# Block B's last output groups as two row halves in two PSUM banks, copied and added by VectorE

## The chip, the cores and the metric

The kernel runs on one NeuronCore of one Trainium2 chip, in one launch. The metric is the device time of that launch in microseconds. Three runs of the kernel before took 1746.45, 1746.89 and 1746.9 us, so the median is 1746.89 us. Five engines work side by side, each through its own queue in order: TensorE (PE, with its weight loads shown as PEld), VectorE (DVE), ScalarE (ACT), GpSimd (POOL), and SyncE (SP), which here only issues DMAs. Engines wait for one another through semaphores. TensorE writes its results to PSUM, which has 8 banks of 512 fp32 columns in each of 128 partitions.

## The reference

Two attention blocks stand side by side, each with 2048 positions, 640 features and 32 heads of 20. Block A attends to 8 positions at a stride of 2; block B is full softmax attention. Cut to what matters for this change, block B is:

```python
qkv = ((x @ wqkv).reshape(B, S, 3, H, Dh)).transpose(2, 0, 3, 1, 4)
q, k, v = qkv[0], qkv[1], qkv[2]
scores = jnp.einsum("bhqd,bhkd->bhqk", q, k) * (Dh ** -0.5)
p = softmax(scores, axis=-1)
o = jnp.einsum("bhqk,bhkd->bhqd", p, v)
return o.transpose(0, 2, 1, 3).reshape(B, S, D) @ wo      # the output projection
```

The change is in the last line, `@ wo`, of block B.

## The kernel before

**Number format.** An fp32 operand of a projection is split into a high and a low part of TensorE's fp32r format (`split`), and a product is three passes: high x high, high x low, low x high (`PASSES`). With 640 features in `KC = 5` chunks of 128, one output group of 128 rows x 320 columns is 15 matmuls that add up in one PSUM bank.

**Stages.** Projections of A and B come first, then the V projections with the first maxima of B, then block B's main loop of 512 steps (`NS`). A step is one group of four heads, one of four query chunks of 512 (`qc`), and one of 16 key blocks of 128. A step has 4 score matmuls (128 keys x 512 queries), 4 exponentials on ScalarE, and 4 value matmuls of 32 output columns each, which put the four heads into four 32-partition strips of one bank (a trace shows each value matmul as two). VectorE takes row maxima for a later step; GpSimd does block A's attention. Of the 512 steps all but the last `TAIL = 24` stand in an order that is written out as a string (`ORDER`). The last 24 are a plain loop at the end of the function: by then VectorE has no maxima left.

**The plain loop.** Each step issues its 8 score and exponential instructions (`b_qk`). Every odd step then issues the value matmuls of two earlier steps (`b_pv`), and takes one waiting job from the list `fill`. These jobs are `out_group(qc, n)`: one 128 x 320 piece of block B's output. Two steps therefore form a period that repeats: 8 score matmuls, 16 value matmuls (as a trace counts them), 15 output matmuls. On ScalarE the period is 8 exponentials, the copy of the value bank into `more` (or `braw`), and the copy of the output bank into `ro` (`store_rows`). SyncE then sends `ro` to `ob`. Jobs that are left over run after the loop, followed by the eight output groups of the last query chunk.

**PSUM banks.** Banks 4 to 7 serve in pairs through `wide()`, and the second half of each step's score matmuls (`pl = 1`) uses them. Banks 0 to 3 are handed out first in, first out:

```python
def bank():
    n = given.pop(0) if given else free.pop(0)
    t = psb[:, n]
    taken[id(t)] = (None if loop[0] is not None and loop[1] else n, t)
    return t

def give(t):
    n = taken.pop(id(t))[0]
    if n is not None:
        free.append(n)
```

`bank()` and `give()` run while the program is written, not on the chip. Each call takes the bank that was taken four calls earlier, and the matmul that writes it gets a semaphore wait for whichever engine reads that older content. In a period, in this order, the first step's scores take two (call them S1 and S2; S3 and S4 are in wide banks), the second step's scores take two (S5 and S6; S7 and S8 are wide), the value matmuls take one, and the output group takes one. So S5 reuses the bank of the last value sum, and S6 that of the last output group.

**Row halves elsewhere.** The V projection already has a form with halves of 64 rows (`v_matmuls` with `r`), where two 64-row matmuls, one on rows 0 to 63 and one on rows 64 to 127, write different banks. Score matmuls also use 62 of 64 rows.

In the profile every recorded instruction has line 71, since the helper class `InOrder` issues them all; they are told apart by tile names: `ps_st` is PSUM, `bq,bk` score matmuls, `e,vb` value matmuls, `ww,xn` and `ww,xl` the projections with 320 columns (output groups, in the plain loop; `xl` is the fifth chunk), `e` exponentials, `ro` output rows.

Of the kernel before, what the change touches and what calls it, by code (L numbers as in the profile page):

```python
# [10 lines left out]
F32 = mybir.dt.float32  # L11
F32R = mybir.dt.float32r
AF = mybir.ActivationFunctionType
ALU = mybir.AluOpType
# [8 lines left out]
KC = 5  # L23
# [7 lines left out]
PASSES = ((0, 0), (0, 1), (1, 0))  # L31
# [7 lines left out]
HALF = 64  # L39
# [3 lines left out]
NS = NG * NQC * NKB  # L43
# [32 lines left out]
def attention_pair(ctx, tc, xa, wqk_a, wv_a, wo_a, xb, wqk_b, wv_b, wo_b, oa, ob):  # L76
# [3 lines left out]
    sb = ctx.enter_context(tc.tile_pool(name="sb", bufs=1))  # L80
    ps = ctx.enter_context(tc.tile_pool(name="ps", bufs=1, space=PS))
    dr = ctx.enter_context(tc.tile_pool(name="dr", bufs=1, space=bass.MemoryType.DRAM))
    pe, dve, act, gp, sp = (InOrder(tc, e) for e in (nc.tensor, nc.vector, nc.scalar, nc.gpsimd, nc.sync))
# [5 lines left out]
    def after(n, fn, *args):  # L89
        due.setdefault(now[0] + n, []).append((fn, args))  # L90
# [32 lines left out]
# [12 lines that stand above are left out]
# [27 lines left out]
    def split(hi, lo, src, tag="stg", second=None, first=None):  # L162

        t = sb.tile([128, 640 if tag == "stg" else 1024], F32, tag=tag, bufs=3 if tag == "stg" else PB, name="stg")
        raw = t[:, :src.free_size()] if len(src.shape) == 2 else (
            t[:, :src.shape[1] * src.shape[2]].rearrange("p (k c) -> p k c", c=src.shape[2]))
        sp.dma_start(raw, src)

        def parts():
            (first or act.copy)(hi, raw)  # L170
            (second or dve).tensor_tensor(lo, raw, hi.bitcast(F32), ALU.subtract)
        after(odd(wait[0]), parts)
# [8 lines left out]
    def chunk(t, xi, k):  # L181
        return t[k // (KC - 1)][:, xi, k % (KC - 1)]
# [90 lines left out]
    def store_rows(p, dst):  # L273
        r = sb.tile([128, 320], F32, tag="r", bufs=4, name="ro")
        act.copy(r, p[:, :320])
        if id(p) in taken:
            give(p)
        after(1, sp.dma_start, dst, r)
# [231 lines left out]
    for n in range(NA):  # L510
        nxt = None
        for t in range(NT):
            if n == 0 and t < 4:
                p = first[t]
            else:
                p = next(banks)
# [64 lines left out]
    for m in range(0, 10, 2):  # L581
        nxt = []
        for n in range(4):
            for j in range(2):
                p = next(banks)
                for k in range(KC):
                    for i, (wi, xi) in enumerate(PASSES):
                        pe.matmul(p, WB[j][:, wi, k], chunk(XB[n], xi, k), start=(k == 0 and i == 0),
                                  stop=(k == KC - 1 and i == 2))
# [154 lines left out]
    def b_qk(i):  # L744
        for pl in range(2):
            w = wide() if pl else None
            ps2 = [bank() for _ in range(2)] if w is None else [w[:, 0], w[:, 1]]
            for r in range(2):
                s_matmul(i, pl, r, ps2[r])
            for r in range(2):  # L750
                s_exp(i, pl, r, ps2[r])
                if w is None:
                    give(ps2[r])

    def b_pv(i):
        u, kb = divmod(i, NKB)
        g, qc = divmod(u, NQC)
        n, part = divmod(kb, 2)
        if part == 0:
            accs[u] = bank()  # L760
        acc = accs[u]
        for j in range(GH):
            pe.matmul(acc[32 * j:32 * j + 32, :], stacks[g][2][:, kb, j * VC:j * VC + 32], P[i][j % 2][:, j // 2],
                      start=(part == 0), stop=(part == 1))
        del P[i]
        if part == 0:
            return
        del accs[u]
        if n == 0:
            raws[u] = sb.tile([128, 512], F32, tag="raw", bufs=3, name="braw")  # L770
            act.copy(raws[u], acc)
        else:
            more = spare[n % 2][:, n // 2 % 2]
            act.copy(more, acc)
            after(2, pool, raws[u], raws[u], more, ALU.add)
        give(acc)
        if kb == NKB - 1:
            last = g == NG - 1
            normalize(raws.pop(u), g, qc * 512, *((2, 3) if last else (5, 8)), (lambda: out_last(qc)) if last else None)
# [64 lines left out]
    outs_b = {}  # L844

    def out_first(qc):

        o = columns(2)
        outs_b[qc] = o
        for k in range(KC - 1):  # L850
            after(1 + 2 * k, split, chunk(o, 0, k), chunk(o, 1, k),
                  ot_b[k * 128:(k + 1) * 128, qc * 512:(qc + 1) * 512], "stg", gp, gp.tensor_copy)

    def out_last(qc):
        o = outs_b[qc]
        k = KC - 1
        split(chunk(o, 0, k), chunk(o, 1, k), ot_b[k * 128:(k + 1) * 128, qc * 512:(qc + 1) * 512])
        if qc < NQC - 1:
            for n in range(8):
                after(3 + (1 + (qc < 2)) * n, fill.append, lambda n=n: out_group(qc, n))  # L860

    def out_matmuls(p, qc, n, ks):
        for k in ks:
            for i, (wi, xi) in enumerate(PASSES):
                pe.matmul(p[:, :320], chunk(outs_b[qc], xi, k)[:, n // 2 * 128:n // 2 * 128 + 128], WO_b[n % 2][wi][:, k],
                          start=(k == 0 and i == 0), stop=(k == KC - 1 and i == 2))

    def out_dst(qc, n):
        r0 = qc * 512 + n // 2 * 128
        return ob[r0:r0 + 128, n % 2 * 320:n % 2 * 320 + 320]  # L870

    def out_group(qc, n):
        p = bank()
        out_matmuls(p, qc, n, range(KC))
        store_rows(p, out_dst(qc, n))
        if n == 7 and qc + 2 < NQC:
            out_first(qc + 2)

# [112 lines left out]
    fill = []  # L991

    WO_b = []
# [4 lines left out]
    def begin(i):  # L998

        g, sub = divmod(i, NQC * NKB)  # L1000
        if sub == (1 if g else 2) and g + 1 < NG:
            k_loads, q_loads = b_pieces(g + 1) if g else ([], q1_loads)
            for n, fn in enumerate(k_loads + q_loads + [lambda g=g + 1: v_piece(g, 0, NKB)]):
                after(1 + (n if n < 8 else 2 * n - 7), fn)
        if i in (NS - 56, NS - 40):
            out_first((i - NS + 56) // NKB)
        tick()
        if loads and (i % 2 or i < 12):
            loads.pop(0)()
        if turn_jobs and turn_jobs[0][0] <= now[0]:  # L1010
            run_jobs(turn_jobs, 1)
        if soft_jobs and soft_jobs[0][0] <= now[0]:
            run_jobs(soft_jobs, 1)
        if done_a and done_a[0][0] <= 0 and len(turned) + len(turn_jobs) < 2 and not loads and i > 10:
            a_turn(*done_a.pop(0)[1:])
        turn_parts()
        gp.us = max(gp.us, (i - 1) * STEP)
        while i >= A_FROM and gp.us < i * STEP + AHEAD:
            if next(a_work, 0) is False:
                break  # L1020
            if not a_work.gi_frame:
                for d in done_a:
                    d[0] -= 1
                break
# [70 lines left out]
    i = 0  # L1095
# [25 lines left out]
    for i in range(NS - TAIL, NS + LAG):  # L1121
        begin(i)
        if i < NS:
            b_qk(i)
        if i % 2:
            b_pv(i - LAG - 1)
            b_pv(i - LAG)
            if fill:
                fill.pop(0)()


    qc = NQC - 1
# [13 lines left out]
    for n, p in enumerate(last):  # L1146
        out_matmuls(p, qc, n, (KC - 1,))
        r = sb.tile([128, 320], F32, tag=("r", "p")[n > 1], bufs=(4, PB)[n > 1], name="ro")
# [38 lines left out]
```

## Time and profile before

| | us |
|---|---|
| median of three runs | 1746.89 |
| profiled execution | 1745.1 |
| its span | 1742.9 |
| PE busy | 1726.1 |
| DVE busy | 1349.3 |
| ACT busy | 1337.3 |
| POOL busy | 1271.9 |
| first and last output group in the plain loop's periods | starts at 1629.9 and 1690.4 |

The span is that of the instructions; the execution takes 2.2 us more than its span. PE is busy 99% of it, but a matmul's row covers its whole stay in a pipelined array, so a busy PE may still be waiting to start the next one; start times tell more. The granted TensorE clock is 1.00 in the windows around the change. In the stretch from 1660 to 1670 us ScalarE is busy 9.43 of 10 us, VectorE 0.00, and GpSimd 1.30.

### The profile page before, as it was taken

To read this page: it belongs to the slowest core of one execution; us is meant where nothing else is said; L and a number is where in the kernel's file an instruction comes from. 1 tells how busy PE (TensorE), PEld (TensorE's weight loads), DVE (VectorE), ACT (ScalarE), POOL (GpSimd) and SP (SyncE) were. 2 spreads that over 40 slices of the span, in tenths; PEclk is the share of its full clock that TensorE was granted. 3 is DMA by queue.
4 is the path that set the end of the run, shared out by engine and by line. 5 is a ranking of instruction groups with operands and counts; after the bars stand their busy time and mean duration, and the time that the engine had idled before them with its cause. 6 is when DMAs were issued, how large, how long until landed. Compare 5 with 4: busy or idle time off the path is not lost.

```text
span 1742.9 us, 34666 instructions
## 1 busy us (share of the span) xinstructions
PE 1726.1 (99%) x12711; PEld 1011.2 (58%) x12711; DVE 1349.3 (77%) x1818; ACT 1337.3 (77%) x2658; POOL 1271.9 (73%) x1125
## 2 busy tenths in 40 slices
PE   9999999999999999999999999999999999999999
PEld 8988888989635544444444443444444445444568
DVE  3113232888899999999999999999999999999300
ACT  4323223232599999999999999999999999999981
POOL 0000950999899999999999999999999953545242
PEclk9999999999999999999999999999999999999999
DMA  6447878657754263445435433543642532111123
GB/s 226 120 139 242 304 258 261 219 183 219 207 152 133 91 175 119 130 127 148 128 121 158 141 126 106 176 136 110 168 137 96 142 90 55 43 36 52 34 75 113
DMA packets 194435, 248.29 MB, mean 142 GB/s; under 512 B 89308, under 2 KB 114396, under 8 KB 193272
## 3 DMA queue, kind: packets, MB, share of 16 engines
q1 hardware_dynamic: 193688, 245.41, 46.6%
q8 instruction: 100, 1.64, 0.4%
q14 instruction: 71, 0.58, 0.1%
q10 hardware_dynamic: 576, 0.66, 0.1%
HBM read 181.08 MB, written 64.91 MB: 141 GB/s over the span
## 4 chain that ended last, share of the span: by engine, by line
PE 73%; POOL 17%; DMA 4%; issue 3%; DVE 2%; ACT 1%; SPq 1%; POOLq 0%; ACTq 0%; DVEq 0%
PE ps_st L71 73%; POOL akv L71 9%; POOL braw L71 4%; DVE mx L71 2%; POOL ao L71 1%; DMA stg<-xa 1%; SPq L71 1%; DMA mdr<-mtr 1%; DMA bq<-qb_d 1%; POOL ww L71 1%; POOL al L71 1%; ACT e L71 1%; DMA s_d<-braw 1%; POOL xn L71 0%; DMA s_d<-sm 0%
## 5 line engine op out<-in xcount | busy, mean ns | idle before, releaser
L71 DVE TENSOR_REDUCE mx<-ps_st 128x1 f32<-128x512 f32 (+1 forms) x1500 | 1227.5, 877 | 72.5 <-PE ps_st L71 61.4
L71 ACT ACTIVATE e<-ps_st 128x512 f32<-128x512 f32 x2048 | 1067.3, 630 | 32.5 <-PE ps_st L71 19.6
L71 PE MATMUL ps_st<-bk,bq 60*128 60x512 f32 x2048 | 555.1, 436 | 0.5 <-DVE mx L71 0.4
L71 PE MATMUL ps_st<-bq,bk 62*128 62x512 f32 x2048 | 548.7, 431 | 3.5 <-ACT e L71 1.8
L71 PE MATMUL ps_st<-e,vb 128*32 128x512 f32 x4096 | 543.1, 604 | 0.5
L71 PEld LDWEIGHTS ps_st<-bq,bk 62*128 62x128 f32 x2048 | 276.6, 184 | 401.6 <-ACT e L71 250.2
L71 POOL TENSOR_TENSOR braw<-braw,more 128x512 f32<-128x512 f32 x224 | 288.3, 1287 | 85.6 <-ACT more L71 85.1
L71 PEld LDWEIGHTS ps_st<-bk,bq 60*128 60x128 f32 x2048 | 257.9, 184 | 102.9 <-DVE mx L71 45.1
L71 POOL TENSOR_TENSOR akv<-akv,aq 128x1280 f32<-128x1280 f32 x64 | 188.4, 2944 | 166.4 <-DMA akv<-ka_d 166.3
L71 POOL TENSOR_TENSOR akv<-akv 128x640 f32<-128x640 f32 (+3 forms) x304 | 282.6, 930 | 14.7
L71 ACT COPY ro<-ps_st 128x320 f32<-128x320 f32 (+2 forms) x172 | 73.9, 465 | 185.9 <-PE ps_st L71 104.0
L71 PE MATMUL ps_st<-ww,xn 64*128 64x320 f32 (+1 forms) x1776 | 188.1, 311 | 6.5 <-POOL xn L71 2.4
L71 PEld LDWEIGHTS ps_st<-ww,xn 64*128 64x128 f32 (+1 forms) x1776 | 175.6, 187 | 22.6 <-ACT e L71 8.3
L71 PEld LDWEIGHTS ps_st<-e,vb 128*32 128x32 f32 x4096 | 82.2, 108 | 149.9 <-issue 77.1
L71 POOL TENSOR_TENSOR akv<-akv,al 128x1280 f32<-128x1280 f32 x64 | 151.6, 2368 | 0.1
L71 ACT COPY more<-ps_st 128x512 f32<-128x512 f32 x224 | 136.7, 610 | 4.0 <-POOL braw L71 2.0
L71 PE MATMUL ps_st<-xn,w 128*128 128x512 f32 x480 | 115.8, 390 | 0.0
L71 PEld LDWEIGHTS ps_st<-xn,w 128*128 128x128 f32 x480 | 90.1, 188 | 19.4
L71 POOL TENSOR_TENSOR xn<-stg,xn 128x512 fp32r<-128x512 f32 (+1 forms) x30 | 53.8, 1804 | 62.8 <-ACT xn L71 61.5
L71 PE MATMUL ps_st<-ww,aot 64*128 64x320 f32 x960 | 99.2, 308 | 0.0
L71 ACT CAST pr<-ps_st 128x512 fp32r<-128x512 f32 x40 | 23.5, 587 | 98.7 <-PE ps_st L71 93.0
L71 PEld LDWEIGHTS ps_st<-ww,aot 64*128 64x128 f32 x960 | 91.0, 186 | 4.6 <-DVE mx L71 0.5
(65 smaller groups left out, 1042.3 us busy)
## 6 DMA issues: line engine op xcount, KB each, us to landing
akv<-ka_d SPq DMA_DIRECT2D x128, 320.0 KB
akv<-va_d SPq DMA_DIRECT2D x128, 320.0 KB
kb_d<-pr SPq DMA_DIRECT2D x20, 512.0 KB
qb_d<-pr SPq DMA_DIRECT2D x20, 512.0 KB
bk<-kb_d SPq DMA_DIRECT2D x16, 640.0 KB
bq<-qb_d SPq DMA_DIRECT2D x64, 160.0 KB
stg<-xb SPq DMA_DIRECT2D x16, 512.0 KB
rb<-s_d SPq DMA_DIRECT2D x128, 64.0 KB
```

The source lines that it names most:

```text
L71: return self.tc.keep_in_program_order(op(*a, **k))
```

## The change

An output group that is taken from `fill` inside the loop while `i < NS` is no longer 15 matmuls of 128 rows into one bank, but 30 matmuls of 64 rows: 15 pairs, of which one half (rows 0 to 63) adds up in one bank and the other (rows 64 to 127) in a second. VectorE copies the first bank into `ro` and then adds the second bank to it. ScalarE's copy of these groups is gone. Both banks are taken before the first matmul and given back after the add has been issued. Groups that run with or after step `NS` keep the old form.

```diff
-                after(3 + (1 + (qc < 2)) * n, fill.append, lambda n=n: out_group(qc, n))
+                after(3 + (1 + (qc < 2)) * n, fill.append, lambda *halves, n=n: out_group(qc, n, *halves))
...
-    def out_group(qc, n):
-        p = bank()
-        out_matmuls(p, qc, n, range(KC))
-        store_rows(p, out_dst(qc, n))
+    def out_group(qc, n, halves=False):
+        if halves:
+            ps2 = [bank(), bank()]
+            for k in range(KC):
+                for i, (wi, xi) in enumerate(PASSES):
+                    for h, p in enumerate(ps2):
+                        rows = slice(h * HALF, h * HALF + HALF)
+                        pe.matmul(p[:, :320], chunk(outs_b[qc], xi, k)[rows, n // 2 * 128:n // 2 * 128 + 128], WO_b[n % 2][wi][rows, k],
+                                  start=(k == 0 and i == 0), stop=(k == KC - 1 and i == 2))
+            r = sb.tile([128, 320], F32, tag="r", bufs=4, name="ro")
+            dve.tensor_copy(r, ps2[0][:, :320])
+            dve.tensor_tensor(r, ps2[1][:, :320], r, ALU.add)
+            for p in ps2:
+                give(p)
+            after(1, sp.dma_start, out_dst(qc, n), r)
+        else:
+            p = bank()
+            out_matmuls(p, qc, n, range(KC))
+            store_rows(p, out_dst(qc, n))
...
-                fill.pop(0)()
+                fill.pop(0)(i < NS)
```

Twelve groups take the new form: one in each of the loop's twelve periods. A period now calls `bank()` seven times instead of six, so the reuse shifts: S1 takes the bank of the last S6, S2 that of the last value sum, S5 that of the first half and S6 that of the second half. The value sum takes the bank of this period's S1, the two halves take those of this period's S2 and S5.

TensorE's queue before, over one period in the plain loop; `x2` counts equal instructions in a row, the brackets name the engine whose semaphore is waited for:

```order
L71 MATMUL ps_st<-ww,xn 128x320 [waits Activation_49]
L71 MATMUL ps_st<-ww,xn 128x320 x11
L71 MATMUL ps_st<-ww,xl 128x320 x3
L71 MATMUL ps_st<-bq,bk 128x512 [waits Activation_49] x2
L71 MATMUL ps_st<-bq,bk 128x512 x2
L71 MATMUL ps_st<-bq,bk 128x512 [waits Activation_49] x2
L71 MATMUL ps_st<-bq,bk 128x512 x2
L71 MATMUL ps_st<-e,vb 32x512 [waits Activation_49]
L71 MATMUL ps_st<-e,vb 32x512 x7
```

And the same place now:

```order
L71 MATMUL ps_st<-ww,xn 128x320 [waits Activation_49] x2
L71 MATMUL ps_st<-ww,xn 128x320 x22
L71 MATMUL ps_st<-ww,xl 128x320 x6
L71 MATMUL ps_st<-bq,bk 128x512 [waits Activation_49] x2
L71 MATMUL ps_st<-bq,bk 128x512 x2
L71 MATMUL ps_st<-bq,bk 128x512 [waits DVE_49] x2
L71 MATMUL ps_st<-bq,bk 128x512 x2
L71 MATMUL ps_st<-e,vb 32x512 [waits Activation_49]
L71 MATMUL ps_st<-e,vb 32x512 x7
```

The 15 output matmuls have become 30, the second of them with a wait of its own, and the second pair of waiting score matmuls (S5 and S6) now waits for VectorE instead of ScalarE.

VectorE's queue now, at the fifth to seventh changed group, with buffer numbers; `xl` is the low part of another chunk and `sm` a reciprocal of softmax sums, which stood there before without the rows of `ro`:

```order
L71 COPY ro_18999<-ps_st_66 128x320 [waits DMAHW0_49,PE_49,Activation_49]
L71 TENSOR_TENSOR ro_18999<-ps_st_66,ro_18999 128x320 [waits DVE_49,PE_49,Activation_49]
L71 TENSOR_TENSOR xl_18271<-stg_18933,xl_18271 128x512 [waits DMAHW5_49,Activation_49]
L71 COPY ro_19067<-ps_st_66 128x320 [waits DMAHW7_49,PE_49]
L71 TENSOR_TENSOR ro_19067<-ps_st_66,ro_19067 128x320 [waits DVE_49,PE_49,Activation_49]
L71 COPY ro_19131<-ps_st_66 128x320 [waits DMAHW0_49,PE_49,Activation_49]
L71 TENSOR_TENSOR ro_19131<-ps_st_66,ro_19131 128x320 [waits DVE_49,PE_49,Activation_49]
L71 RECIPROCAL sm_18966<-sm_18966 128x16 [waits DMAHW1_49]
```

Each add waits for VectorE's own copy before it. SyncE's sends of these twelve `ro` tiles stand where they stood and wait for VectorE instead of ScalarE.

## The prediction

> **What bounds the kernel now.** I read the chain of waits first, cut to the stretch of the change, since it names what the end depends on.
>
> ```profile
> 3 pieces in order of time: start us, us, what
> 1639.67 99.15 PE ps_st L71 x688
> 1738.82 0.02 issue
> 1738.84 0.42 ACT ro L71
> ```
>
> From 1639.67 us to the last copy the end is set by TensorE alone: 688 matmuls in a row, no other engine between them. Whatever delays a matmul in the changed periods therefore delays the end, unless TensorE stood waiting later. So I looked next at the timeline of the last 22 us.
>
> ```profile
> 1721.05 14.24 PE L71 MATMUL ps_st<-ww,xn 128*128 128x320 f32 x96
> 1728.49 0.69 DVE L71 TENSOR_TENSOR xl<-stg,xl 128x512 fp32r<-128x512 f32 x1 [26.35 <-ACT xl L71]
> 1735.12 3.68 PE L71 MATMUL ps_st<-ww,xl 128*128 128x320 f32 x24
> ```
>
> The last chunk (`xl`) is ready at 1728.49 + 0.69 = 1729.18 and is first used at 1735.12: 5.9 us to spare. The transfers behind it start from the value matmuls at the loop's end, so they move with TensorE, and the spare time stays. Nothing there absorbs a delay or a gain.
>
> Then the timeline of one period of two steps, with the two rows that give its length, and the weight load of S6:
>
> ```profile
> 1632.29 1.31 PE L71 MATMUL ps_st<-bq,bk 62*128 62x512 f32 x8
> ...
> 1643.29 1.31 PE L71 MATMUL ps_st<-bq,bk 62*128 62x512 f32 x8
> 1643.39 0.43 ACT L71 COPY ro<-ps_st 128x320 f32<-128x320 f32 x1 [0.57 <-PE ps_st L71]
> 1643.82 4.03 ACT L71 ACTIVATE e<-ps_st 128x512 f32<-128x512 f32 x8
> 1643.87 0.29 PEld L71 LDWEIGHTS ps_st<-bq,bk 62*128 62x128 f32 x3
> 1644.53 1.92 PE L71 MATMUL ps_st<-e,vb 128*32 128x512 f32 x16
> ...
> 1646.38 2.03 PE L71 MATMUL ps_st<-ww,xn 128*128 128x320 f32 x12
> 1647.65 0.67 ACT L71 COPY more<-ps_st 128x512 f32<-128x512 f32 x1
> 1648.25 0.60 PE L71 MATMUL ps_st<-ww,xl 128*128 128x320 f32 x3
> 1648.46 1.29 POOL L71 TENSOR_TENSOR braw<-braw,more 128x512 f32<-128x512 f32 x1 [4.22 <-ACT more L71]
> 1648.78 1.31 PE L71 MATMUL ps_st<-bq,bk 62*128 62x512 f32 x8
> ...
> 1687.27 1.31 PE L71 MATMUL ps_st<-bq,bk 62*128 62x512 f32 x8
> ```
>
> Ten periods lie between the rows at 1632.29 and 1687.27: 5.498 us each. One period is scores 1.24 (1643.29 to 1644.53), values 1.85 (to 1646.38), output group 2.40 (to 1648.78). ScalarE waits 0.57 us in it, so it is not the bound. But see what stands at the seam: the `ro` copy ends at 1643.39 + 0.43 = 1643.82, and the weight load of S6, which reuses the bank that was copied, starts at 1643.87, 0.05 later. Counted from the first score matmul, S6 starts at +0.58. Eight scores spread over 1.24 us would put the sixth at about +0.5 or later anyway. So today the evacuation of the output bank just keeps pace with the scores, with nothing in hand.
>
> **The change, part by part.** All times below are counted from S1's start in the new period.
>
> *ScalarE loses the `ro` copy* (12 x 0.43 = 5.2 us). It is off the chain, since ScalarE had 0.57 us of idle time ahead of each copy. I cost the gain at nothing; the exponentials start with S1's result as before. ScalarE's own period shrinks to 4.03 + 0.67 = 4.7 us, further below TensorE's.
>
> *15 matmuls of 128 rows become 30 of 64 rows.* The V projection shows this form between score matmuls of the same 64-row kind:
>
> ```profile
> 419.74 1.93 PE L71 MATMUL ps_st<-ww,xn 64*128 64x320 f32 x24
> 421.51 0.60 PE L71 MATMUL ps_st<-ww,xl 64*128 64x320 f32 x6
> 421.95 0.69 PE L71 MATMUL ps_st<-bk,bq 60*128 60x512 f32 x4
> ```
>
> Thirty take 421.95 - 419.74 = 2.21 us, so two halves cost what one full matmul costs, about 0.147 us per pair. The present 2.40 us are 15 such slots plus 0.19 for entering from the value matmuls and leaving to the scores. Leaving becomes cheap, as here; entering from the values stays. I take 2.31, halfway, with 2.21 and 2.40 as ends: a gain of 0.09 a period. The Trainium skill says as much (TensorEngine Tiling (Array Packing), Key Properties): switching the tiling mode drains the array, while going from one tile to another of the same mode does not. The change removes one of three switches in a period; by that rule alone, with the whole 0.19 gone, eleven periods would gain 2.1 us, and the rule speaks for the change.
>
> *Two dependent VectorE instructions take the place of one ScalarE copy,* and S5 and S6 wait for them. Their prices:
>
> ```profile
> L71 DVE TENSOR_TENSOR pr<-ps_st,pr 128x512 fp32r<-128x512 f32 x40 | 27.6, 690 | 85.3 <-ACT pr L71 85.3
> L71 DVE TENSOR_TENSOR wd<-stg,wd 128x256 fp32r<-128x256 f32 x6 | 2.5, 418 | 0.0
> L71 DVE COPY ro<-ps_st 128x320 f32<-128x320 f32 x4 | 2.0, 491 | 7.7 <-PE ps_st L71 7.7
> L71 DVE TENSOR_TENSOR ww<-stg,ww 128x320 fp32r<-128x320 f32 x2 | 1.0, 483 | 0.0
> 1624.72 2.36 DVE L71 TENSOR_REDUCE mx<-ps_st 128x2 f32<-128x1024 f32 x2
> 1627.12 0.22 DVE L71 TENSOR_REDUCE mx<-mx 128x16 f32<-128x64 f32 x1
> 1627.13 0.19 PEld L71 LDWEIGHTS ps_st<-bq,bk 62*128 62x128 f32 x2 [0.95 <-DVE mx L71]
> 1627.43 0.21 DVE L71 STREAM_TRANSPOSE mtr<-mx 128x32 f32<-128x32 f32 x1
> ```
>
> The copy has its own row: 0.49. The add has none; the nearest is the 320-column one from SBUF, 0.48, with 0.42 (256 columns) and 0.69 (512 columns, one operand in PSUM as here) as ends. I take 0.48, the same column count. Handing over costs 0.04 from TensorE to the evacuating engine (last output matmul ends 1648.25 + 0.60 = 1648.85; one period earlier the copy started 0.04 after it), 0.09 from one VectorE instruction to a dependent one (1627.34 to 1627.43), and 0.05 from VectorE to TensorE (1627.08 to 1627.13).
>
> Step by step: the last pair of halves ends at 421.51 + 0.60 = 422.11, 0.16 after the first score matmul. So the copy runs from +0.20 to +0.69, and S5 starts at +0.74. The add runs from +0.78 to +1.26, and S6 starts at **+1.31** instead of +0.58. TensorE's queue is in order: behind S6 stand S7, S8 and all value matmuls. From S6 to the values is 0.66 now (1643.87 to 1644.53), so the values start at +1.97, the output group 1.85 later at +3.82, and the next S1 at +3.82 + 2.31 = **+6.13**, against 5.50. That is 0.63 us lost per period.
>
> *The other new waits.* The second half's bank is that of this period's S5, whose exponential is ScalarE's fifth. Eight follow each other at (1647.65 - 1643.82) / 8 = 0.48 us and end 4.03 after the first starts, at +0.53; the fifth ends three slots before that, at +3.1, ahead of +3.82. Hidden. S1 waits for the last S6's exponential and S2 for the copy of the value sum, which start even earlier against the longer period. The `xl` subtraction and the reciprocal on VectorE stand between groups, and VectorE has over 4 us free per period. *SyncE* sends `ro` when the add is done, some 0.7 us later in the period than now, and its later DMAs queue behind that; the earliest that matters is the chunk for the last groups, with the 5.9 us above. *GpSimd* is not touched.
>
> *Sum.* Eleven of the twelve groups are followed by scores; the twelfth is followed by values alone and is costed at nothing (its bank is needed only a group later). 11 x 0.63 = 6.9 us. Profiled span 1742.9 + 6.9 = 1749.8; with the 2.2 us around it the profiled execution would be 1752.0 against 1745.1. The three runs lie 1.8 us above that execution, so the median goes from 1746.89 to **1753.8 us**, 0.4% slower.
>
> *Bounds of that sum.* Low: copy at ScalarE's 0.43, add 0.42, hand-over on VectorE 0.05, output group 2.21. S6 at +1.15 and a period of 5.87: 11 x 0.37 = 4.1 us, 1751.0. High: add 0.69, output group 2.40: a period of 6.43, 11 x 0.93 = 10.2 us, 1757.1.
>
> **Rivals.**
>
> *No new wait (not slower).* If VectorE gave both banks back before S5 and S6 are due, the period would only lose the cheaper exit: 0.09 to 0.19 us, 11 periods, 1744.8 to 1745.9 us. It decides at +0.58: copy and add would have to fit between +0.20 and +0.58. For it speaks an idle VectorE:
>
> ```profile
> 1660.00:1670.00 10.00, 10.00 (x74) 6.00 (x73) 0.00 (x0) 9.43 (x20) 1.30 (x1) 1.00 0.10 35
> ```
>
> Its third busy column, VectorE's, is 0.00 of 10 us there. Against it, that the shortest rows for the two sum to 0.85, and that the written order makes S5 and S6 wait for VectorE. Chance 0.06.
>
> *VectorE held up by GpSimd.* GpSimd's `braw` add runs from 1648.46 to 1649.75, so from -0.32 to +0.97 of the seam, over the whole copy. If the copy waited for it, everything would move by 0.77: 11 x 1.40 = 15.4 us, 1762.3. Against it, the 40 `pr` instructions, of PSUM and SBUF as here, average 0.69 while GpSimd (the fifth busy column) was busy for half of their stage:
>
> ```profile
> 144.00:280.00 136.00, 136.00 (x598) 111.95 (x597) 46.58 (x59) 36.87 (x60) 68.18 (x64) 1.00 0.82 276
> ```
>
> The Trainium skill (SBUF — State Buffer, Who interferes with whom) holds that a VectorE instruction with at most one SBUF input, outside its two-port modes, does not contend with GpSimd. Chance 0.05.
>
> *Halves that do not run side by side.* Thirty at 0.147 each would be 4.4 us, 2.2 more in 12 groups: 26 us on top, about 1780. The rows from 419.74 speak against it. Chance 0.02.
>
> **How the numbers follow.** The forecast gets 0.85 (slower by 0.2% or more in nearly all of its span, whose low end is 4.1 us), the no-wait rival 0.06, GpSimd 0.05, serial halves 0.02, and 0.02 is left for a gain that I do not see. A measurement of this kernel can tell about 0.2%, 3.5 us. Slower: 0.85 less 0.03 for the forecast's low tail, plus 0.07: 0.89. Same: 0.03 + 0.05 = 0.08. Faster: 0.03. The range is 1750.5 to 1757.5, the forecast's bounds with half a microsecond for the spread of the runs (0.45 us).
>
> **What would show it.** In the timeline after: periods of about 6.1 us between the score rows; S6's weight load 0.05 us after each `ro<-ps_st,ro` add and about 1.3 us after S1; copies of 0.49 and adds near 0.48 us on VectorE; pairs of halves 0.147 us apart; ScalarE idle for over 1 us per period; the `xl` of the last chunk still ready well before its use. I am wrong if the periods stay at 5.5 or below (then the scores do not wait), if the add is far from 0.48, or if the time moves in a place before 1629.9, where no instruction has changed.

## The result, and the profile after

Six runs of the changed kernel took 1753.18 to 1755.68 us, with a median of **1754.26 us**. Six runs of the kernel before had a median of 1746.68 us. The ratio is 1.0046 (95% interval 1.0033 to 1.0059), so the change makes the kernel 7.6 us slower. The forecast was 1753.8 us. Further down, one of the ten runs without the add took 1967.09 us at a mean granted clock of 0.78, where every other run of the experiments had 0.995 or more; its time is left out there.

The profiled execution took 1755.68 us with a span of 1753.5; it is the longest of the six. The timeline of one period of the plain loop, from one S1 to the next:

```profile
1641.46 0.63 PE L71 MATMUL ps_st<-bq,bk 62*128 62x512 f32 x4
1641.72 0.49 DVE L71 COPY ro<-ps_st 128x320 f32<-128x320 f32 x1 [5.14 <-PE ps_st L71]
1641.89 4.03 ACT L71 ACTIVATE e<-ps_st 128x512 f32<-128x512 f32 x8 [1.75 <-PE ps_st L71]
1642.27 0.18 PEld L71 LDWEIGHTS ps_st<-bq,bk 62*128 62x128 f32 x1 [0.61 <-DVE ro L71]
1642.35 0.49 DVE L71 TENSOR_TENSOR ro<-ps_st,ro 128x320 f32<-128x320 f32 x1
1642.89 0.29 PEld L71 LDWEIGHTS ps_st<-bq,bk 62*128 62x128 f32 x3 [0.44 <-DVE ro L71]
1643.55 1.93 PE L71 MATMUL ps_st<-e,vb 128*32 128x512 f32 x16
1645.41 2.04 PE L71 MATMUL ps_st<-ww,xn 64*128 64x320 f32 x24
1647.71 0.64 PE L71 MATMUL ps_st<-bq,bk 62*128 62x512 f32 x4
...
1697.63 0.63 PE L71 MATMUL ps_st<-bq,bk 62*128 62x512 f32 x4
```

A period takes 1647.71 - 1641.46 = 6.25 us. On average over nine periods to the last row it is (1697.63 - 1641.46) / 9 = 6.24 us, against 5.50 before. Two weight loads in the middle now wait for VectorE's `ro`: S5's, which begins 0.06 after the copy's end (1642.21), and S6's, 0.05 after the add's end (1642.84). ScalarE's wait in a period, which stood ahead of its `ro` copy with 0.57 us, now stands ahead of the exponentials with 1.75 us, so ScalarE is even further from being the bound.

The chain of waits over that seam (start, length, what; DVEq is VectorE's queue, "issue" is time in which nothing shown was waited for) now goes through VectorE, and TensorE's rows stand only between its pieces:

```profile
1641.72 0.50 DVE ro L71
...
1642.26 0.05 DVEq L71
...
1642.35 0.50 DVE ro L71
...
1642.90 3.22 PE ps_st L71 x24
```

Where 688 matmuls stood in a row before, the end now hangs, in ten of the eleven periods, on 1.2 us of VectorE: a copy, a hand-over of 0.13 (with a piece of VectorE's queue in it), an add, and the hand-overs on both sides. In the eleventh, the one from 1672.65 us, the chain is read through ScalarE, but its timeline shows the same two waits for `ro`.

How much of the difference lies in the changed periods is read from landmarks in both profiles, here those after:

```profile
1635.19 0.63 PE L71 MATMUL ps_st<-bq,bk 62*128 62x512 f32 x4
...
1750.05 0.42 ACT L71 COPY ro<-ps_st 128x320 f32<-128x320 f32 x1 [0.45 <-PE ps_st L71]
```

At the first S1 behind a changed group the changed kernel is 2.9 us late (1635.19 against 1632.29). At the last copy it is 11.2 us late (1750.05 against 1738.84). So 8.3 us arise in the eleven periods. The 2.9 us ahead of them arise where no instruction has changed, and the windows show two stretches where time was lost. The columns are the window, its length, busy time of PE, PEld, DVE, ACT and POOL, the granted clock, and DMA. After:

```profile
376.00:380.00 4.00, 4.00 (x36) 3.81 (x34) 2.36 (x2) 1.81 (x3) 3.69 (x7) 0.57 0.91 286
1630.00:1632.00 2.00, 2.00 (x14) 0.59 (x16) 0.00 (x0) 2.00 (x5) 0.00 (x0) 0.50 0.37 128
```

And before, in the first of them:

```profile
376.00:380.00 4.00, 4.00 (x54) 3.80 (x52) 3.70 (x4) 1.36 (x3) 3.69 (x7) 1.00 0.93 302
```

In these two stretches TensorE's clock was halved: 0.57 on average over 4 us is half the clock for 3.4 us, and from 1630 to 1632 us it is 0.50. Each time some 1.5 us were lost: at 376 us 36 matmuls pass in a window where 54 passed before, and at 1630 us 16 value matmuls take 2.97 us instead of 1.92. Besides, the changed kernel was already 1.0 us late ahead of 376 us and made up as much again between the two stretches. In the profiles of all the experiments below, six of them with the same halves, the clock is 1.00 from 376 to 380 and from 1628 to 1632 us, so these two stretches belong to the single execution and not to the change. They can account for the profile's difference (10.6 us in time) being larger than that of the medians (7.6 us).

### The profile page after: what moved, and what is told of

It reads as the page before. It is cut to its first block, busy times and chain, and to the rows that moved or that the text cites. A ratio compares the mean times of both kernels' runs of the same rounds, so it can differ in the third digit from the quotient of the medians.

```text
span 1753.5 us, 35055 instructions
## 1 busy us (share of the span) xinstructions
PE 1734.9 (99%) x12891; PEld 1014.2 (58%) x12891; DVE 1358.5 (77%) x1842; ACT 1332.5 (76%) x2646; POOL 1272.1 (73%) x1125
## 4 chain that ended last, share of the span: by engine, by line
PE 89%; POOL 4%; DMA 2%; DVE 2%; ACT 1%; issue 1%; SPq 0%; DVEq 0%; POOLq 0%; ACTq 0%
PE ps_st L71 89%; DVE mx L71 2%; POOL akv L71 1%; DMA stg<-wo_a 1%; ACT e L71 1%; DMA qb_d<-pr 1%; DVE ro L71 1%; POOL ww L71 1%; POOL xn L71 0%; POOL ao L71 0%; POOL braw L71 0%; DMA stg<-xa 0%; DMA bq<-qb_d 0%; ACT more L71 0%; POOL al L71 0%
## 5 line engine op out<-in xcount | busy, mean ns | idle before, releaser
L71 PE MATMUL ps_st<-bq,bk 62*128 62x512 f32 x2048 | 555.1, 432 | 6.2 <-DVE ro L71 1.7
L71 ACT COPY ro<-ps_st 128x320 f32<-128x320 f32 (+2 forms) x160 | 68.7, 468 | 180.3 <-PE ps_st L71 101.5
```

What stands on the lines that cost most here:

```text
L71: return self.tc.keep_in_program_order(op(*a, **k))
```

## The experiments

The theory, H: the loss is the serial path through VectorE, a copy, an add and three hand-overs, between the last half and S6. The rivals were M, that 30 matmuls of 64 rows cost more on TensorE than 15 of 128 rows, and C, that the granted clock is lower. A second question was whether the cheaper exit of the halves can be made to count. The kernel before took 1745.77 us on the chip of the first four experiments (19 runs) and 1745.71 us on that of the last four (22 runs).

### The add left out

```diff
             dve.tensor_copy(r, ps2[0][:, :320])
-            dve.tensor_tensor(r, ps2[1][:, :320], r, ALU.add)
```

> The add is left out, so the second half's sum is missing from 12 output groups; its bank has no reader. Theory H (the scores S5 and S6 wait for VectorE to give the two banks back): S5 still starts 0.81 us after S1, S6 right with it instead of at 1.43, the values at about 1.47 instead of 2.09, a period of about 5.64 us instead of 6.26, and 11 x 0.62 = 6.8 us less than the changed kernel: about 1747.5 us. Theory M (the 30 matmuls of 64 rows themselves cost the time): the period stays at 6.26 us and the time at 1754. Theory C (the loss is stretches at half the TensorE clock that the change brings on): the period stays at 6.26 outside such stretches, and the time goes with their number.

Measured: 1746.36 us (median of nine runs), ratio to the kernel before 1.0003 (0.9994 to 1.0013). The timeline:

```profile
1643.38 0.63 PE L71 MATMUL ps_st<-bq,bk 62*128 62x512 f32 x4
1643.65 0.49 DVE L71 COPY ro<-ps_st 128x320 f32<-128x320 f32 x1 [5.15 <-PE ps_st L71]
1644.19 0.30 PEld L71 LDWEIGHTS ps_st<-bq,bk 62*128 62x128 f32 x4 [0.62 <-DVE ro L71]
...
1649.01 0.63 PE L71 MATMUL ps_st<-bq,bk 62*128 62x512 f32 x4
```

The period is 1649.01 - 1643.38 = 5.63 us, 0.62 shorter than with the add. All 30 half matmuls are still there, and so is S5's wait; S6 follows S5 without another wait. One VectorE instruction of 0.49 with its 0.13 of hand-over is therefore worth 0.62 us per period, which is what H expected. The group itself is as long as in the changed kernel, 2.30 us, so M has nothing to explain.

### Whole groups, copied by VectorE

The kernel before, with the same twelve groups of 128 rows in one bank, but VectorE copies them:

```diff
-    def out_group(qc, n):
+    def out_group(qc, n, by_dve=False):
...
-        store_rows(p, out_dst(qc, n))
+        store_rows(p, out_dst(qc, n), dve.tensor_copy if by_dve else act.copy)
```

> The kernel before (15 matmuls of 128 rows, one bank), with only the evacuation of the twelve groups moved from ScalarE to VectorE. H: the copy starts 0.06 us later than ScalarE's and takes 0.49 instead of 0.43, so S6 starts at 0.71 instead of 0.58 and the period grows by 0.13 to 5.63 us: +1.4 us, about 1748. M: period 5.50, no change against before.

Measured: 1746.73 us, ratio 1.0007 (0.9998 to 1.0017), periods of 5.63 us. The timeline:

```profile
1643.49 1.29 POOL L71 TENSOR_TENSOR braw<-braw,more 128x512 f32<-128x512 f32 x1 [4.34 <-ACT more L71]
1643.95 1.45 PE L71 MATMUL ps_st<-bq,bk 62*128 62x512 f32 x8
1644.13 0.49 DVE L71 COPY ro<-ps_st 128x320 f32<-128x320 f32 x1 [5.15 <-PE ps_st L71]
1644.67 0.29 PEld L71 LDWEIGHTS ps_st<-bq,bk 62*128 62x128 f32 x3 [0.20 <-DVE ro L71]
```

S6 starts at 1644.67 - 1643.95 = +0.72 instead of +0.58. Changing only the engine thus costs 0.14 per period: the copy takes 0.49 instead of 0.43, and it starts at +0.18 instead of +0.10. The scores had nothing in hand, as the prediction said, and the periods lengthen by just that. The time cannot show it, since the interval of the ratio holds 1. It also follows that ScalarE's copy was on the path of the kernel before already, although the chain there names TensorE alone from 1639.67 us on; the chain of this run from 1640 to 1650 us names TensorE alone as well. The first row answers a rival: GpSimd's `braw` add runs over this whole copy, and the copy still takes 0.49. The Trainium skill (SBUF — State Buffer, Who interferes with whom) says that a VectorE instruction with at most one SBUF input, outside its two-port modes, does not contend with GpSimd; this row agrees. In the changed kernel `braw` has mostly ended when the copy starts, but once it runs beside both instructions, and copy and add take 0.49 there too:

```profile
1685.40 1.28 POOL L71 TENSOR_TENSOR braw<-braw,rb 128x512 f32<-128x512 f32 x1 [6.38 <-DMA rb<-s_d]
1686.02 0.49 DVE L71 TENSOR_TENSOR ro<-ps_st,ro 128x320 f32<-128x320 f32 x1
```

### One more add

```diff
             dve.tensor_tensor(r, ps2[1][:, :320], r, ALU.add)
+            again = sb.tile([128, 320], F32, tag="r", bufs=4, name="again")
+            dve.tensor_tensor(again, ps2[1][:, :320], r, ALU.add)
```

> The changed kernel with one more VectorE add per group, into a tile that nobody uses, before the second bank is free. H: S6 starts 0.14 + 0.49 = 0.63 us later, at 2.06, the period is 6.89 us and the time 6.9 us above the changed kernel, about 1761. M: VectorE has over 4 us free per period, so nothing moves: period 6.26, 1754.

Measured, a single run: 1757.84 us, with periods of 6.78 us. The chain of waits:

```profile
1645.33 0.50 DVE ro L71
1645.84 0.03 issue
1645.86 0.05 DVEq L71
1645.91 0.04 issue
1645.96 0.50 DVE ro L71
1646.46 0.02 issue
1646.48 0.50 DVE again L71
```

The period grows by 0.53 us, the second add's 0.50 and a hand-over of 0.02. With the run before last the dose reads: no add 5.63, one add 6.25, two adds 6.78. The miss of 0.11 against the expectation is itself a finding: the first add reads what the copy wrote, the second reads what the first wrote, yet one hand-over is 0.12 and the other 0.02. In the written order the first add waits for three semaphores and the second for two, and only the first has a piece of VectorE's queue ahead of it. There the first add's wait for the copy stands in a wait instruction of its own, ahead of the add, while the second add's wait for the first stands in the add itself. That wait instruction may be the piece; no run here separates the place of the wait from the number of waits. The time lies 3 us below the expectation of 1761, of which eleven periods of 0.11 explain 1.2.

### Wide banks first in every second step

In a period's second step the scores of the wide banks go ahead, so that S7 and S8 stand ahead of S5 and S6, which wait for VectorE:

```diff
-        for pl in range(2):
+        for pl in ((1, 0) if i % 2 else (0, 1)):
```

> The changed kernel with the second step's scores in the order S7, S8, S5, S6, so that the two that wait for VectorE stand last. H: S6 still starts at 1.43, but only its own run of 0.42 us lies between it and the values instead of 0.66: period about 6.02 us, 2.6 us less than the changed kernel, about 1751.6. M: no change, period 6.26.

Measured, a single run: 1753.7 us, with periods of 6.17 us. The timeline, at the first two groups:

```profile
1630.49 0.41 PE L71 MATMUL ps_st<-ww,xn 64*128 64x320 f32 x1
1631.18 2.02 PE L71 MATMUL ps_st<-ww,xn 64*128 64x320 f32 x23 [0.28 <-ACT e L71]
...
1637.05 2.33 PE L71 MATMUL ps_st<-ww,xn 64*128 64x320 f32 x24
...
1639.51 1.93 PE L71 MATMUL ps_st<-bq,bk 62*128 62x512 f32 x8
```

The stretch from S1 to the values became 0.24 us shorter, as meant (1.85 us instead of 2.09). But the output group grew to 1639.51 - 1637.05 = 2.46 us, from 2.30. The second half takes S5's bank, and S5's exponential is now ScalarE's seventh instead of its fifth. The first two rows show the wait: one matmul of the first half starts, then the other 23 wait 0.28 us for an exponential. Two thirds of the gain came back as a new wait, and with it the period missed the expectation of 6.02: in a rotation of four banks an order that relieves one reader is late for another.

### The two banks emptied by two engines

ScalarE copies the first half, VectorE copies the second, and GpSimd adds the two in SBUF, off the path:

```diff
-            dve.tensor_copy(r, ps2[0][:, :320])
-            dve.tensor_tensor(r, ps2[1][:, :320], r, ALU.add)
+            r2 = sb.tile([128, 320], F32, tag="r", bufs=4, name="rp")
+            act.copy(r, ps2[0][:, :320])
+            dve.tensor_copy(r2, ps2[1][:, :320])
+            after(1, pool, r, r, r2, ALU.add)
...
-            after(1, sp.dma_start, out_dst(qc, n), r)
+            after(2, sp.dma_start, out_dst(qc, n), r)
```

> The changed kernel's order, with the two halves evacuated side by side: ScalarE copies the first bank, VectorE the second into another tile, and GpSimd adds the two tiles. H: S5 starts at about 0.68 and S6 at 0.81 instead of 1.43, the values at 1.47, a period of about 5.63 us, 1747 to 1748: most of the loss gone, as the two instructions no longer stand one behind the other. M: period 6.26, 1754.

Measured: 1748.01 us, ratio 1.0013 (1.0004 to 1.0022), most periods 5.77 us. The timeline:

```profile
1642.96 1.67 PE L71 MATMUL ps_st<-bq,bk 62*128 62x512 f32 x8
1643.21 0.43 ACT L71 COPY ro<-ps_st 128x320 f32<-128x320 f32 x1 [0.89 <-PE ps_st L71]
1643.36 0.49 DVE L71 COPY rp<-ps_st 128x320 f32<-128x320 f32 x1 [5.28 <-PE ps_st L71]
...
1644.56 1.92 PE L71 MATMUL ps_st<-e,vb 128*32 128x512 f32 x16
```

With the copies side by side most of the loss is gone: the values start at +1.60 instead of +2.09. That fits H. It is not a test of the serial order alone, since the edit also gives the first copy to ScalarE and the add to GpSimd. The period is 0.14 us longer than expected, because ScalarE's copy starts at +0.25 and VectorE's at +0.40. Why so late, the trace does not show. In the written order VectorE's copy now has four waits, where the changed kernel's has two or three; ScalarE's has three as in the kernel before, one of them now for GpSimd.

### Eight banks in rotation, order of the work unchanged

In the plain loop the maxima no longer need the wide pairs. The last 24 steps now take all eight banks first in, first out:

```diff
-            w = wide() if pl else None
+            w = None
...
     loop[1] = False
+    free += range(4, 8)
     for i in range(NS - TAIL, NS + LAG):
...
+    free[:] = [n for n in free if n < 4]
     qc = NQC - 1
```

> The changed kernel with all eight banks first in, first out, but the order of the work as it was. The halves' banks then go to S7 and S8. H: S8 starts at 1.43 as S6 did, with only its own 0.42 us to the values: a period of about 6.0 us, 1751 to 1752. M: 6.26, 1754.

Measured, a single run: 1748.86 us, with periods of 6.02 us. The period is the expected one: with eleven uses of a bank per period and eight banks, the halves' banks go to S7 and S8 instead of S5 and S6, two scores later, and the next S1 moves by only 0.23 us. The time is 2 to 3 us below the expectation. By its landmarks, 5.7 us against the kernel before arise from the first new S1 (1630.98) to the last copy (1743.23), which is what the periods give, but this kernel comes to that first S1 1.3 us earlier than the kernel before (1632.29). The rest is within the spread of single runs.

### Eight banks, and the values between the two score steps

The same, and the value matmuls go ahead of the odd step's scores, so that S5 to S8 stand 2.4 us behind the output group:

```diff
     for i in range(NS - TAIL, NS + LAG):
         begin(i)
-        if i < NS:
-            b_qk(i)
         if i % 2:
             b_pv(i - LAG - 1)
             b_pv(i - LAG)
+        if i < NS:
+            b_qk(i)
+        if i % 2:
             if fill:
                 fill.pop(0)(i < NS)
```

> The changed kernel with two edits in the plain loop: all eight banks are handed out first in, first out, and the value matmuls stand between the two steps' scores (S1 to S4, values, S5 to S8, halves). The halves' banks are then taken by S6 and S7, which start over 2 us after S1, long after copy (0.75) and add (1.38) are done. H: nothing waits for VectorE any more; scores and values lead to S5 at about 2.4, the halves to a period of about 5.2 us: 11 x 1.05 = 11.5 us less than the changed kernel and 3 us less than the kernel before, about 1743. M: the halves keep costing, so at least 5.9 us per period and some 1750.

Measured: **1740.69 us** (1739.73 to 1742.25, 6 runs), ratio to the kernel before **0.9971** (0.9960 to 0.9983). The timeline:

```profile
1642.07 0.63 PE L71 MATMUL ps_st<-bq,bk 62*128 62x512 f32 x4
1642.33 0.49 DVE L71 COPY ro<-ps_st 128x320 f32<-128x320 f32 x1 [4.08 <-PE ps_st L71]
1642.62 1.93 PE L71 MATMUL ps_st<-e,vb 128*32 128x512 f32 x16
1642.95 0.49 DVE L71 TENSOR_TENSOR ro<-ps_st,ro 128x320 f32<-128x320 f32 x1
1644.48 0.73 PE L71 MATMUL ps_st<-bq,bk 62*128 62x512 f32 x4
1645.05 1.92 PE L71 MATMUL ps_st<-ww,xn 64*128 64x320 f32 x24
1647.25 0.63 PE L71 MATMUL ps_st<-bq,bk 62*128 62x512 f32 x4
```

Copy and add are as long as in the changed kernel and start as late (+0.26 and +0.88), but they now lie beside the value matmuls, and no TensorE row waits for VectorE. The period is 1647.25 - 1642.07 = 5.18 us. With the same 30 half matmuls per group this version beats both kernels: it is 5.0 us faster than the one before and, by the two ratios, some 0.7% faster than the changed one. The period is the expected one; the time lies 2 us below the expectation.

### The same two edits on the kernel before

Whole groups of 128 rows copied by ScalarE, eight banks, and the values between the score steps; this tells whether the gain is that of the order or that of the halves.

```diff
-            w = wide() if pl else None
+            w = None
...
+    free += range(4, 8)
...
-        if i < NS:
-            b_qk(i)
...
+        if i < NS:
+            b_qk(i)
```

> The same two edits on the kernel before (15 matmuls of 128 rows, copied by ScalarE). It shows whether a gain of the run with halves comes from the order alone. H: the wait of S6 goes here too, but there are four switches between forms of matmul per period instead of three: about 5.5 us, 1746, no change against before. If the order alone gives the gain: about 5.2 us and 1743.

Measured: 1746.23 us, ratio 1.0004 (0.9995 to 1.0013), periods of 5.58 us. The timeline:

```profile
1640.77 2.02 PE L71 MATMUL ps_st<-ww,xn 128*128 128x320 f32 x12
1643.16 0.73 PE L71 MATMUL ps_st<-bq,bk 62*128 62x512 f32 x4
1643.82 1.92 PE L71 MATMUL ps_st<-e,vb 128*32 128x512 f32 x16
1645.68 0.73 PE L71 MATMUL ps_st<-bq,bk 62*128 62x512 f32 x4
1646.34 1.88 PE L71 MATMUL ps_st<-ww,xn 128*128 128x320 f32 x11
```

Order and banks alone give nothing. ScalarE, which copies here, is not the bound: it waits about 0.4 us ahead of each copy. Set against the version with halves, part by part: the group takes 2.39 us (1643.16 - 1640.77) against 2.20, and the two score stretches 0.66 each against 0.55 and 0.57. The values take 1.86 in both. The difference, 0.39 us per period from these parts, stands where TensorE goes between 128-row groups and 62-row scores, once on each side of the group. So the halves do have a gain, about 0.2 us for each such passage, and in the changed kernel it was buried under the hand-over. Eleven periods of 5.50 - 5.18 = 0.32 are 3.5 us. In the profile the last copy comes 3.9 us earlier than before (1734.90 against 1738.84); the remaining 1.1 us of the medians' 5.0 are not accounted for.

## Why the prediction was right, step by step

- **The mechanism, H, holds.** S5 waits for the copy, S6 for the add, and all that stands behind S6 in TensorE's queue moves with it. The doses confirm it (5.63, 6.25 and 6.78 us with no, one and two adds), and so does their removal from the path: with copy and add beside value matmuls the loss is gone.
- **What bounded the kernel before.** "The end is set by TensorE alone" was read from the chain and left out one thing: ScalarE's copy already set the start of S6, as the copy by VectorE showed (0.14 later, and the period 0.13 longer). The prediction had it right at the seam, with "nothing in hand", though its reason does not hold: eight scores spread evenly over 1.24 us would put the sixth at +0.78, not at about +0.5.
- **Two halves cost what one full matmul costs, and a group takes 2.31.** It took 2.30. The value was chosen halfway between two bounds, so that it came out to 0.01 is in part luck; the versions with eight banks show both ends: 2.20 where the neighbours on both sides are scores, 2.39 for 128 rows between scores.
- **The rule on modes.** The Trainium skill (TensorEngine Tiling (Array Packing), Key Properties) has a change of tiling mode drain the array. The traces agree that fewer changes of mode save time: 0.10 us per period went with the one exit in the changed kernel, 0.39 with two fewer passages between the last two versions. The gain of 2.1 us that the prediction worked out by that rule did not appear in the whole, since it was 0.10 instead of 0.19 us per period and the later S6 took 0.85.
- **Copy 0.49 and add 0.48.** The copy took 0.49, the add 0.49. The 320-column row from SBUF was the right one to take for an add with a PSUM operand.
- **The hand-overs: the mis-sized term.** "Handing over costs 0.04 from TensorE to the evacuating engine", 0.09 from one VectorE instruction to the dependent one. Measured against the last half's modelled end the copy starts after 0.10 (+0.26 instead of +0.20), and the add 0.12 to 0.14 after the copy (+0.89 instead of +0.78). Both prices came from rows of other instructions: a ScalarE copy, and a VectorE transpose behind a reduction. VectorE's copy of whole groups, at +0.18 where ScalarE's stood at +0.10, shows the first price too low by the same amount. S6 came at +1.43 instead of **+1.31** and the next S1 at +6.25 instead of **+6.13**. The loss per period was 0.75 instead of 0.63, and 8.3 us in all instead of 6.9.
- **The forecast in medians** was 7 us and the measurement 7.6, inside the range. That the two lie closer than 8.3 and 6.9 is partly the spread of the runs; before's median plus 8.3 would be 1755.0 us, 0.7 above what was measured.
- **The other waits stayed hidden.** From S6 to the values it is 0.66 us and from there to the group 1.86, as before, so nothing new is waited for in between. The last chunk, on which the "5.9 us to spare" rested, moves with TensorE: its `xl` is ready at 1740.01 + 0.69 = 1740.70 and first used at 1746.33, so 5.6 us are left:

```profile
1740.01 0.69 DVE L71 TENSOR_TENSOR xl<-stg,xl 128x512 fp32r<-128x512 f32 x1 [26.63 <-ACT xl L71]
1746.33 3.68 PE L71 MATMUL ps_st<-ww,xl 128*128 128x320 f32 x24
```

- **The rivals.** "No new wait" fell with the first timeline: copy and add needed until +1.38, and the scores wanted the banks at +0.58. "Halves that do not run side by side" fell with 2.30 us per group. "VectorE held up by GpSimd" fell with the copy of 0.49 beside `braw` in the run with whole groups, and with copy and add of 0.49 beside it at 1685.40 us in the changed kernel.
- **"If the time moves in a place before 1629.9"** was named as a sign of being wrong. In the profiled execution it did move there, by 2.9 us, with two halvings of the clock in unchanged code; the 8.3 us after it are what the forecast is about. See the last section.

## What to carry to other kernels

Before a cheaper form is given more PSUM banks or a longer evacuation, ask which instruction takes each bank next and when: here 1.2 us on VectorE cost 0.75 us per period, because two scores that needed its banks stood right behind the group in TensorE's queue, and cost nothing once 1.9 us of other matmuls stood between. Price a serial hand-over from a row with the same engine and, where the written order shows them, the same waits; 0.02 and 0.12 us are both found in one chain. And when a change loses, look whether its own gain is still there in the parts: the halves' 0.1 to 0.4 us per period was, and another rotation of the banks brought it out.

## What the runs showed of the hardware that was not expected

**The clock halves for about 3.4 us at places that differ from execution to execution.** In the changed kernel's profile this was at 376 and about 1629 us, as shown above. In the kernel with one more add it was at about 492 us, where the window shows:

```profile
492.00:496.00 4.00, 4.00 (x20) 1.96 (x13) 3.10 (x5) 3.54 (x8) 3.76 (x7) 0.57 0.00 0
```

The kernel before, in the same window:

```profile
492.00:496.00 4.00, 4.00 (x26) 1.69 (x22) 3.67 (x5) 4.00 (x10) 3.86 (x4) 1.00 0.00 0
```

Just ahead of it TensorE waits for an exponential in both, 1.71 us with one more add and 1.85 us before, but only the first lost the clock. In this window it is below 1.00 in four of the ten profiles, among them that of whole groups with eight banks (0.67), whose instructions there are those of the kernel before. At 376 us the waits ahead are 1.25 and 0.38 us, at 1629 us 0.33 and 0.64 us, and the kernel before has nearly the same waits there without losing the clock.

The Trainium skill (TensorE: Matmul & The Clock Gate, What's actually happening) describes a monitor with a free-running window of about 3.4 us that lowers the clock by half after an idle window. The length agrees. The cause does not agree as it stands, since in none of the three places is TensorE idle for 3.4 us: the longest wait is 1.71 us. A window whose phase is a matter of chance would fit that the same waits sometimes cost the clock and sometimes not; no run here tested the phase.

The price was about 1.5 us at 376 and at 1629 us, and 0.8 us at 492. So the rival C explains differences of this size between single executions, but not the 0.75 us in each of eleven periods: the clock granted between 1660 and 1670 us was 1.00.

**A dependent VectorE instruction can follow after 0.02 us or after 0.12**, as the chain with one more add shows; the slower one has three waits, one of them for the copy in an instruction of its own, and the quicker one two. Which of these makes the difference was not tested.

**A passage between 128-row groups and 62-row scores costs about 0.2 us on TensorE**, of which 0.1 shows in the group and 0.1 in the scores.
